# An fnet-plus-gMLP block in split fp32: a new opening for the first three x tiles, three mod rows spread by fp32r products, and the last operands' chain overlapped

## The chip, the cores and the metric

The kernel runs on one core of one Trainium2 chip. The metric is the device time of one execution in microseconds (us), the median of three runs. One further execution is recorded by the hardware profiler; all positions in time below are in us from the start of that execution's span.

## The reference, cut to what matters

```python
mod = (silu(c) @ w_mod).reshape(1, 6, 1, 512)        # w_mod: 512 x 3072
sa, ca, ga, sb, cb, gb = mod rows 0..5
h = layernorm(x) * (1 + ca) + sa                     # x: 2048 x 512
a = h @ dft_hid_re.T;  b = h @ dft_hid_im.T          # 512 x 512 each
x = x + ga * (dft_seq_re @ a - dft_seq_im @ b)       # 2048 x 2048 each
h = layernorm(x) * (1 + cb) + sb
z = gelu(h @ w_in);  z1, z2 = halves of z            # 512 x 1792
g = w_sp @ layernorm(z2) + b_sp[:, None]             # w_sp: 2048 x 2048
out = x + gb * ((z1 * g) @ w_out)                    # w_out: 896 x 512
```

Everything is fp32.

## The kernel before

Each large fp32 product is made of three fp32r products: an operand is split into a high part (`hi`, a copy rounded to fp32r on ScalarE) and a low part (`lo`, the difference, on VectorE), and `matmul3` sums hi x hi, lo x hi and hi x lo in one PSUM bank. Lines L79, L80 and L81 are these three products; each streams 512 columns against a 128 x 128 stationary block.

The large matrices arrive as blocks of 512 x 512 (`stage`, 1 MB, two buffers, loaded by four DMAs of SyncE's queue). A quarter of a block is called a step here, and numbered n. For step n, `prep_hi` makes the transposed tile `t` on VectorE (L142) and `ah` on ScalarE (L165), and `prep_lo` makes `al` on VectorE (L174). `prep(n)` runs three steps ahead with the hi part and two steps ahead with the lo part. There are two `t`, four `ah` and three `al` buffers, so an `al` for step n waits until TensorE has ended step n - 3.

In the first pass (steps 0 to 31) a step is 12 products of 128 x 512: `gp<-ah,hh`, `gp<-al,hh` and `gp<-ah,hl` for each of four banks. `hh` and `hl` are the hi and lo part of one tile of 128 rows of the modulated layernorm, called tile s below (in the profile `x`, `xn`, `hh`, `hl` with its number). Steps 0 to 3 use tiles 0 to 3 with the cosine block, steps 4 to 7 the same tiles with the sine block, steps 8 to 11 and 12 to 15 tiles 4 to 7, and so on: a new group of four tiles is needed from steps 8, 16 and 24 on, one tile a step.

Such a tile goes through `stats_x` (mean and variance on VectorE, L87 and L89; then three small operations on GpSimd, L91, L92 and L99), `norm_x` (ScalarE, L103), `scale_x` (times mod row 1, L255), `shift_x` (plus mod row 0, L258), `hi_h` (ScalarE, L266) and `lo_h` (VectorE, L271). For tiles 4 to 15 the scale and the shift run on GpSimd.

The six mod rows are sums over four chunks of w_mod (`wm`, 128 x 512 each). Rows 1 and 0 are needed first and are summed by fp32 products with `scb` (silu(c) spread over 128 columns, L225). The others are summed on VectorE by `sum_mod`, and `make_mod` (L231) spreads the sum over all partitions by one fp32 product with `ones`; the profile records such a product as two instructions. `keep_mod` (L207) copies the row out of PSUM.

In the last stage the gate `g` (L464) is added and multiplied into `u` (L466, on GpSimd for even f and on VectorE for odd f), split into `uh` and `ul` (L75, L76), and multiplied with `wo` into four banks `op`, for f from 0 to 6: 12 products each.

The order on every engine is the order in which the code issues it (no scheduler moves it). `at(n, f, ...)` queues a call that `run(n)` makes after step n's products were issued. An engine works its instructions off in that order, so one that waits holds up what stands behind it.

Of the kernel before, what the change touches and what calls it, by code (L numbers as in the profile page):

```python
# [19 lines left out]
def fnet_gmlp_kernel(  # L20
# [45 lines left out]
    def bank(k, name):  # L66
        return psum.tile([P, 512], F32, tag=f"bank{k}", bufs=1, name=name)
# [5 lines left out]
    def split(hi, lo, src):  # L73

        nc.scalar.activation(hi, src, AF.Copy)  # L75
        nc.vector.tensor_tensor(lo, src, hi.bitcast(F32), op=ALU.subtract)  # L76
# [30 lines left out]
    def at(n, f, *a):  # L107
        fill.setdefault(n, []).append((f, a))
# [44 lines left out]
    def prep_hi(n):  # L153
        if n >= NE:
            return
        b, k = divmod(n, 4)
        T[n] = blocks.tile([P, Q], F32, tag="t", bufs=2, name=f"t{n}")
        if N3 <= n < N4:

            nc.vector.transpose(T[n].rearrange("p (k a i) -> p a k i", k=4, i=32),  # L160
                                stage[b][:, :, 32 * k:32 * k + 32].rearrange("p (a k) i -> p a k i", k=4))
        else:
            squares(T[n], stage[b], k)
        AH[n] = blocks.tile([P, Q], F32R, tag="ah", bufs=4, name=f"ah{n}")
        nc.scalar.activation(AH[n], T[n], AF.Copy)  # L165
        if k == 3:
            stage.pop(b)
            load(b + 2)

    def prep_lo(n):  # L170
        if n >= NE:
            return
        AL[n] = blocks.tile([P, Q], F32R, tag="al", bufs=3, name=f"al{n}")
        nc.vector.tensor_tensor(AL[n], T.pop(n), AH[n].bitcast(F32), op=ALU.subtract)  # L174
# [17 lines left out]
    sc = cpool.tile([P, ND], F32, name="sc")  # L192
    nc.scalar.activation(sc, ccol, AF.Silu)
    scb = spool.tile([P, ND, P], F32, name="scb")
    for k in range(ND):
        nc.vector.tensor_scalar(scb[:, k, :], ones, sc[:, k:k + 1], None, op0=ALU.mult)
    wm, mods = {}, {}

    def load_mod(j):
        wm[j] = [SP[-1].tile([P, D], F32, tag=f"wm{k}", bufs=2 if len(SP) == 1 else 1, name=f"wm{j}_{k}") for k in range(ND)]  # L200
        for k in range(ND):
            nc.sync.dma_start(wm[j][k], w_mod[k * P:(k + 1) * P, j * D:(j + 1) * D])

    def keep_mod(j, ps, pl, plus_one):
        if j not in mods:
            mods[j] = pl.tile([P, D], F32, name=f"mod{j}")
        nc.scalar.activation(mods[j], ps, AF.Copy, bias=1.0 if plus_one else 0.0)  # L207

    def sum_mod(j, ks=range(4), pl=None):
        w = wm[j]  # L210
        for k in ks:
            if k == 0:
                nc.vector.tensor_scalar(w[0], w[0], sc[:, 0:1], None, op0=ALU.mult)
            else:
                d = w[0]
                if k == 3 and pl:
                    d = mods[j] = pl.tile([P, D], F32, name=f"mod{j}")
                nc.vector.scalar_tensor_tensor(d, w[k], sc[:, k:k + 1], w[0], op0=ALU.mult, op1=ALU.add)

    def sum_mod_first(j, k, pl, plus_one):  # L220

        ps = bank(k, f"modp{j}")
        w = wm.pop(j)
        for m in range(ND):
            nc.tensor.matmul(ps, scb[:, m, :], w[m], start=m == 0, stop=m == ND - 1)  # L225
# [10 lines left out]
    def load_x(g, ks=range(4)):  # L236

        if g not in XG:
            XG[g] = spool.tile([P, 4, D], F32, tag="x", bufs=2, name=f"x{g}")
        k0, k1 = ks[0], ks[-1] + 1  # L240
        v = x.rearrange("(g a k i) d -> g a i k d", g=NQ, a=4, i=32)
        for a in range(4):
            nc.sync.dma_start(XG[g][32 * a:32 * a + 32, k0:k1, :], v[g, a][:, k0:k1, :])
        for k in ks:
            X[4 * g + k] = XG[g][:, k, :]

    def stats_x(s):
        NRM[s] = norm([X[s]], "x")

    def norm_x(s):  # L250
        LN[s] = spool.tile([P, D], F32, tag="xn", bufs=4, name=f"xn{s}")
        apply(LN[s], X.pop(s), NRM.pop(s))

    def scale_x(s, eng=nc.vector):
        eng.tensor_tensor(LN[s], LN[s], mods[1], op=ALU.mult)  # L255

    def shift_x(s, eng):
        eng.tensor_tensor(LN[s], LN[s], mods[0], op=ALU.add)  # L258
# [5 lines left out]
    def hi_h(s):  # L264
        h_hi[s] = hpool.tile([P, ND, P], F32R, name=f"hh{s}")
        nc.scalar.activation(*parts_h(s, h_hi), AF.Copy)  # L266

    def lo_h(s):
        h_lo[s] = hpool.tile([P, ND, P], F32R, name=f"hl{s}")
        lo, h = parts_h(s, h_lo)  # L270
        nc.vector.tensor_tensor(lo, h, parts_h(s, h_hi)[0].bitcast(F32), op=ALU.subtract)  # L271
        LN.pop(s)
# [229 lines left out]
            mm([n])  # L502


    load_x(0, range(2))
    load_mod(1)
    load_mod(0)
    load(0)
    load_x(0, range(2, 4))
    load(1)  # L510
    load_x(1)
    stats_x(0)
    stats_x(1)
    norm_x(0)
    norm_x(1)
# [12 lines left out]
    prep_lo(1)
    lo_h(1)
    stats_x(2)  # L530
    stats_x(3)
    norm_x(2)
    norm_x(3)
    scale_x(2)
    shift_x(2, nc.gpsimd)
# [195 lines left out]
```

## Time and profile before

| | us |
|---|---|
| median of three runs | 1011.55 (1011.09 to 1011.59) |
| the profiled execution, its time | 1010.55 |
| the profiled execution, its span | 1008.8 |
| outside the span | 1.75 |
| first product of step 0 | 18.47 |
| first product of the last stage | 983.99 |
| last product | 1004.42 |

A timeline row gives the start and the duration in us, the engine (PE is TensorE's matmul, PEld its weight load, DVE VectorE, ACT ScalarE, POOL GpSimd, SPq SyncE's DMA queue), the line, the operation, output and inputs, and in brackets how long the engine had been idle and what ended that wait. The durations of neighbouring matmuls overlap, so the pace of TensorE is read from start to start.

### The profile page before, as it was taken

How to read it: one execution, taken by the hardware profiler on the slowest of the kernel's cores; microseconds unless marked ns; L12 is line 12 of the kernel's file. 1: busy time of each engine (PE TensorE's matmuls, PEld its weight loads, DVE VectorE, ACT ScalarE, POOL GpSimd, SP SyncE). 2: the span in 40 equal slices, each digit the busy share in tenths (PEclk: the TensorE clock that was granted, in tenths of full speed). 3: DMA queues.
4: the chain of work that ended last, by engine and by line, in shares of the span. 5: the costliest groups of instructions: out<-in, count | busy, mean ns of one | idle time of the engine just before them, and what ended most of it. 6: DMA issues, size and time to landing. Idle time of an engine off the chain costs nothing.

```text
span 1008.8 us, 11594 instructions
## 1 busy us (share of the span) xinstructions
PE 989.4 (98%) x4344; PEld 817.5 (81%) x4344; DVE 530.6 (53%) x810; ACT 293.0 (29%) x447; POOL 177.3 (18%) x285
## 2 busy tenths in 40 slices
PE   5899999999999999999999999999999999999998
PEld 3678888788888888888888998888888888888886
DVE  4777874666565545647432676565332632263315
ACT  2444441322232313222442675431111111111101
POOL 2677002022310023004321112102000200020001
PEclk9999999999999999999999999999999999999999
DMA  9674962565354353555553232425225222521141
GB/s 241 134 168 106 207 150 70 136 157 146 94 125 97 81 136 105 123 117 156 181 201 142 42 67 60 115 60 150 72 62 157 53 63 66 154 68 48 42 136 42
DMA packets 145961, 114.28 MB, mean 113 GB/s; under 512 B 7024, under 2 KB 125808, under 8 KB 145904
## 3 DMA queue, kind: packets, MB, share of 16 engines
q1 hardware_dynamic: 139296, 93.61, 39.7%
q0 software_dynamic: 6080, 19.93, 5.4%
q8 instruction: 34, 0.56, 0.2%
q14 instruction: 23, 0.19, 0.1%
q10 hardware_dynamic: 528, 0.00, 0.0%
HBM read 93.59 MB, written 19.92 MB: 113 GB/s over the span
## 4 chain that ended last, share of the span: by engine, by line
PE 90%; POOL 4%; DVE 2%; issue 1%; ACT 1%; DMA 0%; SPq 0%; POOLq 0%; DVEq 0%; ACTq 0%
PE gw L79 10%; PE gw L81 10%; PE gw L80 10%; PE gp L81 10%; PE gp L80 10%; PE gp L79 10%; PE yp L81 3%; PE yp L80 3%; PE yp L79 3%; PE z2p L80 3%; PE z2p L79 3%; PE z2p L81 3%; PE z1p L79 3%; PE z1p L81 3%; PE z1p L80 3%; PE op L81 2%
## 5 line engine op out<-in xcount | busy, mean ns | idle before, releaser
L165 ACT ACTIVATE ah<-t 128x512 fp32r<-128x512 f32 x224 | 141.4, 631 | 547.7 <-PE gw L81 212.2
L174 DVE TENSOR_TENSOR al<-t,ah 128x512 fp32r<-128x512 f32 x224 | 156.1, 697 | 271.8 <-PE gw L80 142.3
L79 PE MATMUL gp<-ah,hh 128*128 128x512 f32 x512 | 202.7, 396 | 7.1 <-ACT ah L165 4.1
L80 PE MATMUL gp<-al,hh 128*128 128x512 f32 x512 | 201.3, 393 | 2.2 <-DVE al L174 2.2
L81 PE MATMUL gp<-ah,hl 128*128 128x512 f32 x512 | 200.8, 392 | 0.2 <-DVE hl L271 0.2
L81 PE MATMUL gw<-ah,zl 128*128 128x512 f32 x448 | 174.5, 389 | 0.0
L80 PE MATMUL gw<-al,zh 128*128 128x512 f32 x448 | 174.5, 389 | 0.0
L79 PE MATMUL gw<-ah,zh 128*128 128x512 f32 x448 | 174.5, 389 | 0.0
L142 DVE STREAM_TRANSPOSE t<-stage 128x512 f32<-128x512 f32 x208 | 146.3, 703 | 5.1 <-DMA stage<-in_A_dft_seq_re_dram 1.5
L79 PEld LDWEIGHTS gp<-ah,hh 128*128 128x128 f32 x512 | 96.9, 189 | 29.5 <-ACT ah L165 4.9
L80 PEld LDWEIGHTS gp<-al,hh 128*128 128x128 f32 x512 | 97.0, 189 | 24.6 <-DVE al L174 4.1
L81 PEld LDWEIGHTS gp<-ah,hl 128*128 128x128 f32 x512 | 97.0, 189 | 21.2 <-DVE hl L271 1.3
L81 PEld LDWEIGHTS gw<-ah,zl 128*128 128x128 f32 x448 | 84.1, 188 | 17.6
L80 PEld LDWEIGHTS gw<-al,zh 128*128 128x128 f32 x448 | 84.1, 188 | 17.4
L79 PEld LDWEIGHTS gw<-ah,zh 128*128 128x128 f32 x448 | 84.1, 188 | 17.3
L466 POOL TENSOR_TENSOR u<-u,g 128x512 f32<-128x512 f32 x16 | 20.7, 1291 | 343.4 <-DVE g L464 343.4
L337 POOL DMA_DIRECT2D x_d<-xr x16 | 8.8, 548 | 246.6 <-DVE xr L336 246.6
L81 PE MATMUL yp<-hth,gl 128*128 128x512 f32 x128 | 49.9, 389 | 0.0
L79 PE MATMUL yp<-hth,gh 128*128 128x512 f32 x128 | 49.8, 389 | 0.0
L80 PE MATMUL yp<-htl,gh 128*128 128x512 f32 x128 | 49.8, 389 | 0.0
L80 PE MATMUL z2p<-wil,ah 128*128 128x448 f32 x128 | 46.8, 366 | 0.0
L81 PE MATMUL z2p<-wih,al 128*128 128x448 f32 x128 | 46.8, 366 | 0.0
(94 smaller groups left out, 1158.4 us busy)
## 6 DMA issues: line engine op xcount, KB each, us to landing
stage<-in_A_dft_seq_re_dram SPq DMA_DIRECT2D x64, 256.0 KB, 5.1
stage<-in_A_dft_seq_im_dram SPq DMA_DIRECT2D x64, 256.0 KB, 5.1
stage<-in_B_w_sp_dram SPq DMA_DIRECT2D x64, 256.0 KB, 4.9
stage<-h_d SPq DMA_DIRECT2D x32, 256.0 KB, 4.7
z_d<-z POOLq DMA_DIRECT2D x28, 256.0 KB, 5.8
u<-z_d SPq DMA_DIRECT2D x4, 1792.0 KB, 8.0
wm<-in_w_mod_dram SPq DMA_DIRECT2D x24, 256.0 KB, 4.6
xr<-in_A_x_dram POOLq DMA_DIRECT2D x16, 256.0 KB, 3.3
```

Of the source, the lines that this page charges most:

```text
L79: nc.tensor.matmul(acc, ah, bh, start=first, stop=False)
L80: nc.tensor.matmul(acc, ah, bl, start=False, stop=False)
L81: nc.tensor.matmul(acc, al, bh, start=False, stop=last)
L142: nc.vector.transpose(dst.rearrange("p (b i) -> p b i", i=32), block[:, :, 32 * k:32 * k + 32])
L165: nc.scalar.activation(AH[n], T[n], AF.Copy)
L174: nc.vector.tensor_tensor(AL[n], T.pop(n), AH[n].bitcast(F32), op=ALU.subtract)
L337: nc.gpsimd.dma_start(x2_d[t][i * P:(i + 1) * P, :], x2)
L466: eng.tensor_tensor(U[t][:, f, :], U[t][:, f, :], g, op=ALU.mult)
```

## The change

The diff does five things.

1. The first DMA brings three x tiles instead of two. Tiles 0, 1 and 2 go together through statistics, `norm_x`, scale and shift, all four shifts and scales on VectorE; tile 3 is made by `make_x` out of two fused operations on VectorE (with its own statistics), without ScalarE and GpSimd's wide operations.
2. Mod row 0 is summed in part on VectorE: three of its chunks by `sum_mod`, the fourth by TensorE with `scb`, and the VectorE sum is added by a product with `ones`. Two products of constants stand on TensorE ahead of mod row 1 and three behind mod row 0 (`keep_busy`); nothing reads their output.
3. From tile 4 on the statistics start at the steps of the list `begin`, most of them unchanged, those of tiles 4 to 7 one or two steps later; the scale and shift are issued with `norm_x` instead of a step later, and hi and lo three steps after the statistics.
4. Mod rows 4, 3 and 5 are split into hi and lo (`split_mod`) and spread by two fp32r products (`spread_mod`) instead of one fp32 product. Mod row 2 keeps `make_mod`.
5. In the last stage the gate, the multiplication and `uh` of f + 1 are issued ahead of `ul` and the products of f.

```diff
-    def sum_mod_first(j, k, pl, plus_one):
+    def sum_mod_first(j, k, pl, plus_one, summed=0):
 
         ps = bank(k, f"modp{j}")
         w = wm.pop(j)
-        for m in range(ND):
-            nc.tensor.matmul(ps, scb[:, m, :], w[m], start=m == 0, stop=m == ND - 1)
+        for m in range(summed, ND):
+            nc.tensor.matmul(ps, scb[:, m, :], w[m], start=m == summed, stop=not summed and m == ND - 1)
+        if summed:
+            nc.tensor.matmul(ps, ones, w[0], start=False, stop=True)
+        keep_mod(j, ps, pl, plus_one)
+
+    def keep_busy(n, k):
+
+        ps = bank(k, "busyp")
+        for _ in range(n):
+            nc.tensor.matmul(ps, ones, busy, start=True, stop=True)
+
+    def split_mod(j):
+        w = wm[j][0]
+        wm[j] = [SP[-1].tile([P, D], F32R, tag=f"ws{i}", bufs=1, name=f"ws{j}_{i}") for i in range(2)]
+        split(*wm[j], w)
+
+    def spread_mod(j, k, pl, plus_one):
+
+        ps = bank(k, f"modp{j}")
+        hi, lo = wm.pop(j)
+        nc.tensor.matmul(ps, ones_r[0], hi, start=True, stop=False)
+        nc.tensor.matmul(ps, ones_r[0], lo, start=False, stop=True)
         keep_mod(j, ps, pl, plus_one)
...
+    def make_x(s):
+
+        mean, rstd = stats([X[s]], "x")
+        LN[s] = spool.tile([P, D], F32, tag="xn", bufs=4, name=f"xn{s}")
+        nc.vector.scalar_tensor_tensor(LN[s], X.pop(s), mean, mods[1], op0=ALU.subtract, op1=ALU.mult)
+        nc.vector.scalar_tensor_tensor(LN[s], LN[s], rstd, mods[0], op0=ALU.mult, op1=ALU.add)
...
-    load_x(0, range(2))
+    load_x(0, range(3))
     load_mod(1)
     load_mod(0)
     load(0)
-    load_x(0, range(2, 4))
+    load_x(0, range(3, 4))
     load(1)
     load_x(1)
...
+    keep_busy(2, 5)
...
+    sum_mod(0, range(3))
     sum_mod_first(1, 7, spool, True)
-    sum_mod_first(0, 6, spool, False)
-    scale_x(0)
+    sum_mod_first(0, 6, spool, False, 3)
+    keep_busy(3, 5)
...
-    for s in range(4, NS):
-        at(max(2 * s - 9, 2), stats_x, s)
-        at(max(2 * s - 8, 3), norm_x, s)
-        at(max(2 * s - 7, 3), scale_x, s, nc.gpsimd)
-        at(max(2 * s - 7, 3), shift_x, s, nc.gpsimd)
-        at(max(2 * s - 5, 4), split_h, s)
+    begin = [3, 4, 5, 7, 9, 11, 13, 15, 17, 19, 21, 22]
+    for s, n in zip(range(4, NS), begin):
+        at(n, stats_x, s)
+    for s, n in zip(range(4, NS), begin):
+        at(n + 1, norm_x, s)
+        at(n + 1, scale_x, s, nc.gpsimd)
+        at(n + 1, shift_x, s, nc.gpsimd)
+        at(n + 3, split_h, s)
...
+        at(n + 2, split_mod, j)
-        at(n + 4, make_mod, j, k, cpool if j == 5 else htpool, plus_one)
+        at(n + 4, spread_mod, j, k, cpool if j == 5 else htpool, plus_one)
...
-    for f in range(NF):
+    def first_part(f):
         make_u(t, f)
         uh[f] = blocks.tile([P, Q], F32R, tag="ah", bufs=4, name=f"uh{f}")
+        nc.scalar.activation(uh[f], U[t][:, f, :], AF.Copy)
+
+    first_part(0)
+    for f in range(NF):
+        if f + 1 < NF:
+            first_part(f + 1)
         ul[f] = blocks.tile([P, Q], F32R, tag="al", bufs=3, name=f"ul{f}")
-        split(uh[f], ul[f], U[t][:, f, :])
+        nc.vector.tensor_tensor(ul[f], U[t][:, f, :], uh[f].bitcast(F32), op=ALU.subtract)
```

How the order moves, first on VectorE at the start, from the first scale (before) and from the last two sums of mod row 0 (changed) on. `xn1` is tile 1, `mod1` a mod row, `wm0_0` the running sum of mod row 0, `t0` and `al0` belong to step 0. Before:

```order
L255 TENSOR_TENSOR xn0_171<-xn0_171,mod1_180 128x512
L258 TENSOR_TENSOR xn0_171<-xn0_171,mod0_187 128x512
L255 TENSOR_TENSOR xn1_173<-xn1_173,mod1_180 128x512
L271 TENSOR_TENSOR hl0_195<-xn0_171,hh0_193 128x512
L142 STREAM_TRANSPOSE t0_197<-stage0_134 128x512
L174 TENSOR_TENSOR al0_201<-t0_197,ah0_199 128x512
L142 STREAM_TRANSPOSE t1_203<-stage0_134 128x512
L174 TENSOR_TENSOR al1_209<-t1_203,ah1_205 128x512
L271 TENSOR_TENSOR hl1_211<-xn1_173,hh1_207 128x512
```

The same place with the change:

```order
L220 SCALAR_TENSOR_TENSOR wm0_0_128<-wm0_1_129,sc_106,wm0_0_128 128x512
L220 SCALAR_TENSOR_TENSOR wm0_0_128<-wm0_2_130,sc_106,wm0_0_128 128x512
L278 TENSOR_TENSOR xn0_185<-xn0_185,mod1_199 128x512
L278 TENSOR_TENSOR xn1_187<-xn1_187,mod1_199 128x512
L278 TENSOR_TENSOR xn2_189<-xn2_189,mod1_199 128x512
L281 TENSOR_TENSOR xn0_185<-xn0_185,mod0_204 128x512
L281 TENSOR_TENSOR xn1_187<-xn1_187,mod0_204 128x512
L301 TENSOR_TENSOR hl0_219<-xn0_185,hh0_214 128x512
L281 TENSOR_TENSOR xn2_189<-xn2_189,mod0_204 128x512
L301 TENSOR_TENSOR hl1_222<-xn1_187,hh1_217 128x512
L142 STREAM_TRANSPOSE t0_224<-stage0_136 128x512
L174 TENSOR_TENSOR al0_228<-t0_224,ah0_226 128x512
```

Between the copy of mod row 0 and `t0`, five wide operations stand where three stood; the shifts of tiles 1 and 2 are among them, where before GpSimd made them.

Second, on VectorE around `al8`, the lo operand of step 8. Before:

```order
L271 TENSOR_TENSOR hl4_401<-xn4_355,hh4_399 128x512
L142 STREAM_TRANSPOSE t8_405<-stage2_247 128x512
L174 TENSOR_TENSOR al7_409<-t7_372,ah7_374 128x512
L271 TENSOR_TENSOR hl5_425<-xn5_359,hh5_423 128x512
L87 BN_STATS bstx_429<-x1_148 128x6
L89 BN_AGGR mvx_431<-bstx_429 128x2
L142 STREAM_TRANSPOSE t9_438<-stage2_247 128x512
L174 TENSOR_TENSOR al8_442<-t8_405,ah8_407 128x512
```

With the change:

```order
L142 STREAM_TRANSPOSE t8_393<-stage2_258 128x512
L174 TENSOR_TENSOR al7_397<-t7_353,ah7_355 128x512
L87 BN_STATS bstx_411<-x1_150 128x6
L89 BN_AGGR mvx_413<-bstx_411 128x2
L142 STREAM_TRANSPOSE t9_424<-stage2_258 128x512
L174 TENSOR_TENSOR al8_428<-t8_393,ah8_395 128x512
L301 TENSOR_TENSOR hl4_444<-xn4_389,hh4_442 128x512
L142 STREAM_TRANSPOSE t10_450<-stage2_258 128x512
L174 TENSOR_TENSOR al9_454<-t9_424,ah9_426 128x512
L87 BN_STATS bstx_468<-x1_150 128x6
L89 BN_AGGR mvx_470<-bstx_468 128x2
L301 TENSOR_TENSOR hl5_479<-xn5_420,hh5_477 128x512
```

`al8` stood behind `hl5`, and now stands ahead of `hl4`.

Third, on VectorE in the last stage (`g3_1` is the gate of f = 1, `ul0` the lo part of f = 0). Before:

```order
L464 TENSOR_TENSOR g3_0_7696<-gw3_0_7148,bs3_7576 128x512
L76 TENSOR_TENSOR ul0_7700<-u3_7574,uh0_7699 128x512
L464 TENSOR_TENSOR g3_1_7715<-gw3_1_7149,bs3_7576 128x512
L466 TENSOR_TENSOR u3_7574<-u3_7574,g3_1_7715 128x512
L76 TENSOR_TENSOR ul1_7719<-u3_7574,uh1_7718 128x512
L464 TENSOR_TENSOR g3_2_7738<-gw3_2_7150,bs3_7576 128x512
```

With the change:

```order
L494 TENSOR_TENSOR g3_0_7720<-gw3_0_7172,bs3_7600 128x512
L494 TENSOR_TENSOR g3_1_7725<-gw3_1_7173,bs3_7600 128x512
L496 TENSOR_TENSOR u3_7598<-u3_7598,g3_1_7725 128x512
L731 TENSOR_TENSOR ul0_7730<-u3_7598,uh0_7723 128x512
L494 TENSOR_TENSOR g3_2_7744<-gw3_2_7174,bs3_7600 128x512
L731 TENSOR_TENSOR ul1_7749<-u3_7598,uh1_7728 128x512
```

The gate of f + 1 moves ahead of the lo part of f, throughout the stage.

More of the change, by code (lines that the diff above doesn't have):

```diff
@@ L194, in fnet_gmlp_kernel @@
     scb = spool.tile([P, ND, P], F32, name="scb")
+    busy = spool.tile([P, D], F32, name="busy")
+    nc.vector.memset(busy, 1.0)
     for k in range(ND):
@@ L508, in fnet_gmlp_kernel @@
     load(0)
-    load_x(0, range(2, 4))
+    load_x(0, range(3, 4))
     load(1)
     load_x(1)
[L512 to L515, printed above, removed]
+    keep_busy(2, 5)
+    for s in range(3):
+        stats_x(s)
+    for s in range(3):
+        norm_x(s)
+    sum_mod(0, range(3))
     sum_mod_first(1, 7, spool, True)
-    sum_mod_first(0, 6, spool, False)
-    scale_x(0)
+    sum_mod_first(0, 6, spool, False, 3)
+    keep_busy(3, 5)
+    for s in range(3):
+        scale_x(s)
     shift_x(0, nc.vector)
-    scale_x(1)
-    shift_x(1, nc.gpsimd)
     hi_h(0)
+    shift_x(1, nc.vector)
+    hi_h(1)
     lo_h(0)
+    shift_x(2, nc.vector)
+    lo_h(1)
     prep_hi(0)
     prep_lo(0)
+    hi_h(2)
     prep_hi(1)
-    hi_h(1)
     prep_lo(1)
[L529 to L535, printed above, removed]
+    lo_h(2)
+    make_x(3)
     prep_hi(2)
-    scale_x(3)
-    shift_x(3, nc.gpsimd)
-    at(0, split_h, 2)
     at(0, hi_h, 3)
@@ L556, in change_pools @@
         load_ht(1)
+    ones_r = []
     def change_spool():
@@ L561, in change_spool @@
         load_mod(4)
+        ones_r.append(SP[-1].tile([P, P], F32R, name="ones_r"))
+        nc.scalar.activation(ones_r[0], ones, AF.Copy)
     at(14, load_mod, 2)
```

## The prediction

> **What bounds the kernel.** I read the page, then the waits, then the timeline of TensorE alone.
>
> ```profile
> PE 989.4 (98%) x4344; PEld 817.5 (81%) x4344; DVE 530.6 (53%) x810; ACT 293.0 (29%) x447; POOL 177.3 (18%) x285
> ```
>
> TensorE is busy for 98% of the span, so only three things can save time: a wait of TensorE, a stretch at its lower clock, or a product that costs less. Its waits (engine and line, what it waited for: total us, times, longest):
>
> ```profile
> PE modp L225 <- DMA wm<-in_w_mod_dram: 5.8, 1, 5.8
> PE gp L79 <- ACT ah L165: 4.1, 1, 4.1
> PE gp L79 <- ACT hh L266: 3.0, 1, 3.0
> PE gp L80 <- DVE al L174: 2.2, 3, 1.3
> ```
>
> All of them are in the opening. The next rows are TensorE's there: the mod sums, the first product of steps 0, 2, 3 and 8, the second of step 8, the first and third of step 11, and the first of steps 12, 19 and 28.
>
> ```profile
> 5.82 8.56 PE L225 MATMUL modp<-wm,scb 128*128 128x512 f32 x16 [5.82 <-DMA wm<-in_w_mod_dram]
> 18.47 0.49 PE L79 MATMUL gp<-ah,hh 128*128 128x512 f32 x1 [4.08 <-ACT ah L165]
> 29.21 0.79 PE L79 MATMUL gp<-ah,hh 128*128 128x512 f32 x1 [2.99 <-ACT hh L266]
> 33.67 0.39 PE L79 MATMUL gp<-ah,hh 128*128 128x512 f32 x1
> 47.29 0.39 PE L79 MATMUL gp<-ah,hh 128*128 128x512 f32 x1
> 49.03 0.50 PE L80 MATMUL gp<-al,hh 128*128 128x512 f32 x1 [1.34 <-DVE al L174]
> 57.23 0.50 PE L79 MATMUL gp<-ah,hh 128*128 128x512 f32 x1
> 58.12 0.50 PE L81 MATMUL gp<-ah,hl 128*128 128x512 f32 x1 [0.15 <-DVE hl L271]
> 60.52 0.39 PE L79 MATMUL gp<-ah,hh 128*128 128x512 f32 x1
> 79.56 0.39 PE L79 MATMUL gp<-ah,hh 128*128 128x512 f32 x1
> 104.44 0.39 PE L79 MATMUL gp<-ah,hh 128*128 128x512 f32 x1
> ```
>
> Undisturbed, a step takes (79.56 - 60.52) / 7 = 2.72 us, or 0.2267 a product. Step 2 lasts 4.46 instead, step 8 loses 1.5, step 11 takes 3.29 (0.57 lost), and steps 19 to 27 lose 104.44 - 79.56 - 9 x 2.72 = 0.40. The clock explains step 2 (columns: window, length, busy us of PE, PEld, DVE, ACT, POOL; granted clock, DMA share, GB/s):
>
> ```profile
> 20.00:22.00 2.00, 2.00 (x6) 1.52 (x6) 1.54 (x3) 0.95 (x2) 0.00 (x0) 0.50 1.21 228
> 26.00:29.00 3.00, 0.22 (x1) 0.00 (x0) 2.61 (x4) 1.92 (x4) 2.07 (x2) 1.00 0.10 25
> 31.00:33.00 2.00, 2.00 (x7) 1.54 (x6) 2.00 (x5) 0.83 (x2) 0.00 (x0) 0.58 1.15 220
> ```
>
> After each long idle time the clock is about half for some 3 to 4 us.
>
> **Part 1, the opening.** The goal is the moment when step 3 can start, 33.67 before. I follow the new chain.
>
> *Mod row 0.* Its last chunk decides. Below are the last two `wm` DMAs (starts of the issue, then time to landing), and DVE's rows at the start.
>
> ```profile
> L202 SPq DMA_DIRECT2D wm<-in_w_mod_dram x2: 430/430/430, 5.4 to 5.9; - x2
> DMA to landing us min/median/max: 5.6/6.0/6.4
> 14.42 0.60 ACT L207 ACTIVATE mod<-modp 128x512 f32<-128x512 f32 x1 [2.84 <-PE modp L225]
> 15.05 0.69 DVE L258 TENSOR_TENSOR xn<-xn,mod 128x512 f32<-128x512 f32 x1 [2.74 <-ACT mod L207]
> 15.66 0.68 DVE L255 TENSOR_TENSOR xn<-xn,mod 128x512 f32<-128x512 f32 x1
> 18.45 0.69 DVE L174 TENSOR_TENSOR al<-t,ah 128x512 fp32r<-128x512 f32 x1 [0.70 <-ACT ah L165]
> 223.52 0.75 DVE L218 SCALAR_TENSOR_TENSOR wm<-wm,sc,wm 128x512 f32<-128x512 f32 x1
> ```
>
> The chunks landed at 11.0 and 12.3. A third x tile stands ahead of them on SP's queue: 262 KB more. At the 228 GB/s of the window from 20 to 22 that is 1.15 us. The two last chunks are 0.26 MB each and landed 1.3 apart, but the six before them came faster: issued 0.43 apart, they landed by 11.0, 1.8 MB and 0.5 MB of x in the 9 us from 2 on, 260 GB/s or 1.0 us; some of that time is latency. I take 0.75, between none and 1.15: the last chunk lands at 13.05. VectorE's sum is ready at 11.75 + 0.75 = 12.5, in time. Two fp32 products follow on TensorE, 0.87 each at full clock (part 2): 1.7, and 0.15 to the last product's end, on which the copy waits. It starts at 14.9 and ends at 15.55, against 15.0 before. So mod row 0 comes 0.5 later, not sooner. Mod row 1, the idle products (covered by the 5.8 us wait for the first chunk, and by the 4 us before step 0) and the three scales all end before that.
>
> *VectorE from 15.55 on.* A wide operation follows the last after 0.61 (15.05 to 15.66); `al0` and `al1` each wait 0.70 for ScalarE. To `t0`: five operations ahead and itself, 6 x 0.61 plus 0.3 for `hh0`, to 19.55. It starts at 18.85, 1.8 later than before (18.45 less 0.70 and its own 0.70), so block 0, which the extra tile delays by at most 1.15 on SP's queue, is covered; the blocks and tiles behind it on that queue keep their sum of bytes. `al0` ends 1.4 later, `t1` and `al1` another 2.0: 22.95. Then `hl2`, the statistics of tile 3 (0.61 + 0.69 + 0.18), two fused operations (1.5), `t2`, `t3` and `al2` (1.95): 27.95. TensorE starts step 0 at 20.3 instead of 18.47. Steps 0 and 1 took 7.6 us from there to the end in the trace, at half clock, so they end at 27.9, and at full clock at about 25.9. In both cases `al2` lets step 2 go on at 28.0, now without the 3 us idle time ahead. Step 3 starts at 28.0 + 11 x 0.2267 = 30.5: **3.2 sooner.**
>
> *Step 8.* `al8` waited behind `hl5`, which waited for tile 5 from GpSimd. It now stands ahead of `hl4`; the 1.5 us go. Step 11 would start at 30.5 + 8 x 2.72 = 52.25.
>
> *Step 11 and after.* Tile 7's lo part is next to be late, through GpSimd.
>
> ```profile
> 35.80 0.55 POOL L92 TENSOR_TENSOR rsx<-mvx,mhalf 128x1 f32<-128x1 f32 x1
> 67.30 1.30 POOL L255 TENSOR_TENSOR xn<-xn,mod 128x512 f32<-128x512 f32 x1 [0.93 <-ACT xn L103]
> 68.67 1.62 POOL L258 TENSOR_TENSOR xn<-xn,mod 128x512 f32<-128x512 f32 x1
> 70.66 0.89 POOL L92 TENSOR_TENSOR rsx<-mvx,mhalf 128x1 f32<-128x1 f32 x1
> 72.83 1.29 POOL L255 TENSOR_TENSOR xn<-xn,mod 128x512 f32<-128x512 f32 x1 [0.93 <-ACT xn L103]
> ```
>
> One tile takes GpSimd 5.53 (67.30 to 72.83): 3.0 for scale and shift, 1.1 to 1.5 for the small operations, 0.9 waiting for ScalarE. Tile 5's statistics stand behind `al6`, which waits for the end of step 3 (33.2): GpSimd has them at 34.9 and, as its order puts both small chains ahead of tile 4's scale, is through with tile 4 at 39.0, with tiles 5 and 6 at 46.1 (one small chain, two wide pairs), with tile 7 at 51.2; up to 52.2 if every L92 takes 0.89. `hh7` and `hl7` add 1.4: 52.6 to 53.6, against 52.7 when step 11's third product is due. The loss is 0 to 0.95; I take 0.5, near the 0.57 of before. Step 12 then starts at 52.25 + 2.72 + 0.5 = 55.5, which is 5.0 sooner. From there four tiles cost GpSimd 22.1 and TensorE 21.8, so at steps 19 and 27 up to 0.36 is lost each, 0.7 against 0.40 before. **The opening gives 4.7.** Ends: 3.5 (the 1.2 us load, and 0.95 at step 11) and 5.7 (no later load, no loss at step 11).
>
> **Part 2, three mod rows.** The product before, the mod product, and the second product after it; then `al` of step 51.
>
> ```profile
> 190.40 0.39 PE L81 MATMUL gp<-ah,hl 128*128 128x512 f32 x1
> 190.63 1.02 PE L231 MATMUL modp<-wm,ones 128*128 128x512 f32 x2
> 191.72 0.39 PE L80 MATMUL gp<-al,hh 128*128 128x512 f32 x1
> 188.58 0.65 DVE L174 TENSOR_TENSOR al<-t,ah 128x512 fp32r<-128x512 f32 x1
> ```
>
> The row costs 1.32 - 2 x 0.2267 = 0.87. Two fp32r products of the usual shape cost 0.45, so 0.41 is saved, three times: **1.2** (none, if a split came late). Each split adds 0.6 to ScalarE and 0.7 to VectorE. The tightest is the first: `al` of step 51 ended at 189.2 and is used at 191.72, 2.5 us of cover against 0.7 plus as much waiting for ScalarE.
>
> **Part 3, the last stage.** Its first product, two places where TensorE waited, and its last; VectorE's lo part at the first of these places.
>
> ```profile
> 983.99 0.39 PE L79 MATMUL op<-woh,uh 128*128 128x512 f32 x1
> 995.34 0.69 DVE L76 TENSOR_TENSOR ul<-u,uh 128x512 fp32r<-128x512 f32 x1 [2.07 <-ACT uh L75]
> 995.36 0.50 PE L79 MATMUL op<-woh,uh 128*128 128x512 f32 x1
> 1001.51 0.50 PE L79 MATMUL op<-woh,uh 128*128 128x512 f32 x1
> 1004.42 0.39 PE L81 MATMUL op<-woh,ul 128*128 128x512 f32 x1
> ```
>
> 84 products need 83 x 0.2267 = 18.8 from first to last; they took 20.4. VectorE has five operations for two f (3.4 us) while TensorE has 24 products (5.4), so issued one f ahead the chain gate, GpSimd, `uh`, `ul` keeps up; what remains is TensorE. I take **1.4** of the 1.6; ends 0.8 (half) and 1.6. The additions and stores behind the last product stay as they are.
>
> **Sum.** 4.7 + 1.2 + 1.4 = 7.3. The profiled execution goes from 1010.55 to 1003.25. The median of the runs shown lies 1.0 above it, so I predict 1004.3.
>
> [...] The clock decides the two fp32 products of mod row 0: at half clock they take 3.4 instead of 1.7. TensorE is idle ahead of them from the end of mod row 1 (four products of 0.87 from 5.82 + 0.75 on, at full clock to 10.05; a chunk may hold up the last one a little) to 13.05, at most 3.0 us. The trace: 2.99 us of idle time were enough for the half clock from 29.21 on. [...]
>
> **Rivals.** *Half clock at mod row 0.* For it speaks the 2.99 us that were enough at 29.21; against it, that the window from 26 to 29 still shows a clock of 1.00, so the drop came only at the very end of that idle time. Everything up to step 28 comes 1.7 later: 1006.0.
>
> *The opening is no sooner.* The change delays step 0, and if `al2` came at 31.1 instead of 27.95 step 3 would start at 33.67 again. That needs 3.2 us more on VectorE, more than any row shows; the reordering at step 8 would still pay. Without the 3.2: 1007.5; without both, 1009.
>
> *Slower: GpSimd becomes the bound.* Before, it was through with tile 11 at 75.8 (72.83 + 3.0), 2.8 ahead of the third product of step 19 less 1.4 for `hh` and `hl`; now it has nothing to spare from tile 7 on. Each 0.1 us on its 5.53 costs 0.8 over the eight tiles from 8 to 15. From 6.45 us a tile on the whole gain is gone; at 6.9 the kernel takes 1015.3. Against it: L92 moved by only 0.34 when other engines were active, and no row of GpSimd's wide operations moved by more.
>
> *Better:* the third tile costs the mod loads nothing and tile 7 is in time: 1003.3 or less.
>
> **Chances.** The forecast (1003.3 to 1005.4) 0.55; half clock 0.23; better 0.12; no sooner 0.07; GpSimd-bound 0.03. The range that leaves out no more than 2 in 10 runs from 1002.4 to 1007.0. A change of 0.2% (2.0 us) is about what a measurement of this kernel can tell from none: faster than that 0.94, same 0.03, slower 0.03.
>
> **What would show it.** Step 0 at about 20.3, step 3 at about 30.5 without a bracketed wait of 3 us ahead of step 2; no wait at step 8; the third product of step 11 behind `hl` L301; two L247/L248 products at 0.23 each; 18.8 to 19.0 from first to last product of the last stage. Wrong would be above all a mod row 0 copied later than 16, an `al2` later than 29, or GpSimd's tiles more than 5.6 apart.

## The result, and the profile after

The changed kernel takes 1003.13 us (median; 1002.91 to 1003.54) against 1011.37 us (1011.09 to 1011.59) for the kernel before on the same chip: ratio 0.9919, 95% interval [0.9902, 0.9936]. The two profiled executions took 1003.15 and 1010.55 us, 7.4 us apart.

The page's first row, and the rows of TensorE's own waits (engine and line, what it waited for: total us, times, longest):

```profile
PE 988.9 (99%) x4350; PEld 818.5 (82%) x4350; DVE 543.1 (54%) x820; ACT 295.9 (30%) x450; POOL 172.9 (17%) x281
PE modp L227 <- DMA wm<-in_w_mod_dram: 3.2, 2, 1.7
PE gp L79 <- ACT ah L165: 2.7, 1, 2.7
```

The wait for `hh` (3.0) ahead of step 2 is gone, and so is the 1.34 us wait for `al` at step 8. Now the timeline of TensorE: the start of mod row 0's two products, the idle products, the first products of steps 0, 2, 3, 9, 10, 11, 12 and 28, the two products of one spread mod row, and the first and last product of the last stage.

```profile
12.21 1.12 PE L227 MATMUL modp<-wm,scb 128*128 128x512 f32 x2 [1.66 <-DMA wm<-in_w_mod_dram]
14.03 2.74 PE L236 MATMUL busyp<-busy,ones 128*128 128x512 f32 x6
19.48 0.80 PE L79 MATMUL gp<-ah,hh 128*128 128x512 f32 x1 [2.72 <-ACT ah L165]
28.27 0.39 PE L79 MATMUL gp<-ah,hh 128*128 128x512 f32 x1
30.99 0.39 PE L79 MATMUL gp<-ah,hh 128*128 128x512 f32 x1
47.31 0.39 PE L79 MATMUL gp<-ah,hh 128*128 128x512 f32 x1
50.03 0.39 PE L79 MATMUL gp<-ah,hh 128*128 128x512 f32 x1
53.26 0.50 PE L79 MATMUL gp<-ah,hh 128*128 128x512 f32 x1 [0.35 <-ACT hh L296]
56.41 0.39 PE L79 MATMUL gp<-ah,hh 128*128 128x512 f32 x1
99.98 0.39 PE L79 MATMUL gp<-ah,hh 128*128 128x512 f32 x1
186.13 0.39 PE L247 MATMUL modp<-ws,ones_r 128*128 128x512 f32 x1
186.36 0.39 PE L248 MATMUL modp<-ws,ones_r 128*128 128x512 f32 x1
978.19 0.39 PE L79 MATMUL op<-woh,uh 128*128 128x512 f32 x1
997.00 0.39 PE L81 MATMUL op<-woh,ul 128*128 128x512 f32 x1
```

Read against the rows of before: step 3 starts 2.68 us sooner (33.67 to 30.99), step 9 4.34 sooner (51.65 to 47.31: step 8's stall is gone), step 12 4.11 sooner (60.52 to 56.41), step 28 4.46 sooner. A spread row is two products of 0.227 us, 0.455 in all, against 0.87. The last stage takes 18.81 from first to last product instead of 20.43. That is nearly the whole difference of 7.4 us: 4.46 + 3 x 0.415 + 1.62 = 7.3.

The row that matters most is the one at 28.27. It has no bracket: TensorE came to step 2 busy. The third `al` had ended at 27.60, 0.67 earlier (first row), and the clock tells why TensorE was late (columns as in the windows of before; the clock is the third number from the end):

```profile
26.91 0.69 DVE L174 TENSOR_TENSOR al<-t,ah 128x512 fp32r<-128x512 f32 x1
19.00:19.50 0.50, 0.02 (x1) 0.02 (x1) 0.04 (x1) 0.50 (x2) 0.00 (x0) 0.64 1.27 227
20.00:25.00 5.00, 5.00 (x12) 3.84 (x12) 3.79 (x8) 0.63 (x1) 1.05 (x2) 0.50 1.07 224
25.50:26.00 0.50, 0.50 (x3) 0.41 (x2) 0.50 (x2) 0.00 (x0) 0.00 (x0) 0.53 0.09 25
```

Half clock lasted from 19.14 to 25.97 (0.64 is the mean of the window from 19.00 to 19.50, so its first 0.14 us were at full clock; the end in the same way), and steps 0 and 1 took 8.79 us (19.48 to 28.27). In that stretch products follow each other 0.43 us apart (21.23, 21.65, 22.08), behind it 0.227. The prediction had reckoned with 7.6 at the most, and with `al2` as the bound.

### The profile page after: what moved, and what is told of

Its sections match the earlier page's. It is cut to its first block, busy times and chain, and to the rows that moved or that the text cites. A ratio compares the mean times of both kernels' runs of the same rounds, so it can differ in the third digit from the quotient of the medians.

```text
span 1001.4 us, 11608 instructions
## 1 busy us (share of the span) xinstructions
PE 988.9 (99%) x4350; PEld 818.5 (82%) x4350; DVE 543.1 (54%) x820; ACT 295.9 (30%) x450; POOL 172.9 (17%) x281
## 4 chain that ended last, share of the span: by engine, by line
PE 94%; POOL 2%; issue 1%; DVE 1%; DMA 1%; ACT 0%; SPq 0%; DVEq 0%; POOLq 0%
PE gp L81 11%; PE gp L80 11%; PE gp L79 10%; PE gw L79 10%; PE gw L81 10%; PE gw L80 10%; PE yp L81 3%; PE yp L80 3%; PE yp L79 3%; PE z2p L80 3%; PE z2p L79 3%; PE z2p L81 3%; PE z1p L79 3%; PE z1p L80 3%; PE z1p L81 3%; PE op L81 2%
## 5 line engine op out<-in xcount | busy, mean ns | idle before, releaser
L174 DVE TENSOR_TENSOR al<-t,ah 128x512 fp32r<-128x512 f32 x224 | 161.6, 721 | 271.6 <-PE gw L80 142.6
L79 PE MATMUL z2p<-wih,ah 128*128 128x448 f32 x128 | 46.7, 365 | 0.0
```

The costliest lines, as they stand in the source:

```text
L79: nc.tensor.matmul(acc, ah, bh, start=first, stop=False)
```

## Experiments

First theory, the prediction's: VectorE's chain from mod row 0 to `al2` lets step 2 go on, whatever the clock is; beside it, the order at step 8 and GpSimd at step 11. Second theory, from the trace after: TensorE at half clock bounds steps 0 to 2, with `al2` right behind it. Each kernel was timed beside the kernel before, whose median moved between 1011.37 and 1012.11; each ratio's interval is about 0.0015 (1.5 us) to either side, so that for differences of 1 or 2 us between two changed kernels the traces decide and the times only agree or not.

### The three parts by themselves

`open_only` is the change without the spread rows and without the new last stage; `mod_only` and `tail_only` are the kernel before with one of these.

> Only the opening of the change (three x tiles first, mod row 0 partly summed on VectorE, idle products, the new order up to step 19); mod rows 3 to 5 and the last stage as before. By the prediction's terms, as the changed kernel's trace corrects them: the opening gives 4.5 of 7.4 us, so 1.2 + 1.6 = 2.8 above the changed kernel: 1005.9. If the parts hide each other (what comes sooner at step 28 waits again later): less far above it, 1004 to 1005.

> Only the three mod rows of the change (split into two fp32r tiles and spread by two products); the opening and the last stage as before. By the rows of the two traces a spread row costs TensorE 0.455 instead of 0.87 us: 3 x 0.41 = 1.2 less than the kernel before, 1010.2, and the two rows of each pair stand 0.23 apart without a wait. If the splits hold up the operands' chain on VectorE once the opening's 4.5 us have not moved the work there: a wait ahead of the pairs and less than 1.2.

> Only the last stage of the change (the chain of the next f issued one f ahead); the opening and the mod rows as before. By the rows of the two traces 1.6 us: 1011.4 - 1.6 = 1009.8. If the last stage's gain needs the work that the other parts moved: no change, 1011.4.

Measured: `open_only` 1005.80 us (ratio 0.9940 [0.9927, 0.9952]), `mod_only` 1010.33 (0.9988 [0.9979, 0.9998]), `tail_only` 1009.80 (0.9982 [0.9973, 0.9990]). The savings 6.0, 1.2 and 1.8 thousandths add up to 9.0, against 8.1 for the whole, within the intervals: as far as these times can tell, the parts neither need nor hide each other. The rows give the small ones more exactly. The first product of a spread row of `mod_only` and the product behind the row, 0.46 later without a wait; then the ends of the last stage of `tail_only`, 18.82 apart:

```profile
191.09 0.39 PE L237 MATMUL modp<-ws,ones_r 128*128 128x512 f32 x1
191.55 0.39 PE L79 MATMUL gp<-ah,hh 128*128 128x512 f32 x1
984.84 0.39 PE L79 MATMUL op<-woh,uh 128*128 128x512 f32 x1
1003.66 0.39 PE L81 MATMUL op<-woh,ul 128*128 128x512 f32 x1
```

### The clock or `al2`: two edits, alone and together

`long_busy`:

```diff
     sum_mod_first(0, 6, spool, False, 3)
-    keep_busy(3, 5)
+    keep_busy(6, 5)
```

`early_al2`:

```diff
     prep_hi(0)
+    prep_hi(1)
     prep_lo(0)
     hi_h(2)
-    prep_hi(1)
     prep_lo(1)
     lo_h(2)
-    make_x(3)
     prep_hi(2)
+    at(0, make_x, 3)
     at(0, hi_h, 3)
```

`early_long` is both.

> The changed kernel with six idle products instead of three behind mod row 0 (twelve halves of 0.43 us instead of six, about 14.0 to 19.2 us). First theory, the prediction's: the third al (al2, ended at 27.60) lets step 2 go on, whatever the clock is; then this kernel takes the time of the changed kernel, 1003.1, give or take 0.3. Second theory, from the changed kernel's trace: TensorE's half clock from 19.5 to 25.9 us made steps 0 and 1 take 8.79 us and bounds step 2 itself; with the clock up step 2 waits only for ah2 and al2 (26.9 and 27.6), step 3 starts at about 30.1 instead of 30.99, 0.9 sooner: 1002.3. Third: the steps at full clock end at 25.0, TensorE then idles for 2.4 us before step 2 and loses the clock there, where 2.72 us of idle time were enough for it before step 0; step 2 at half clock takes 5.4 us, step 3 starts at 32.8 or later, 1.8 later: 1004.9.

> The changed kernel with VectorE's opening in another order: t0 and t1 ahead of al0 and al1 (which takes away its two waits of 0.70 us for ScalarE), and t2, t3 and al2 ahead of the statistics and the two fused operations of tile 3. By the durations of the changed kernel's rows al2 then ends at about 24.8 us instead of 27.60, and the hi and lo parts of tile 3 at about 28.2 and 29.5. Idle products as in the changed kernel. First theory (al2 bounds step 2, the clock does not): step 2 goes on 2 us or more sooner; step 3 then waits for tile 3 and starts at 28.6 to 29.2 instead of 30.99: about 1001. Second theory (TensorE at half clock bounds steps 0 and 1): step 2 still starts at about 28.2 and, at a full clock from 25.9 on, step 3 at 30.9: 1003.1, or up to 0.8 less where step 1 no longer waits for al1.

> Both edits together: six idle products instead of three behind mod row 0, and VectorE's opening reordered so that al2 ends at about 24.8 us. Second theory (both the half clock and, right behind it, al2 bound the opening): neither edit alone brings more than 0.9, both together bring more than the sum: step 0 at 19.5, steps 0 and 1 at full clock to 25.0, step 2 to 27.7, step 3 from 28.3 with its third product behind the lo part of tile 3 at 29.5: step 4 at about 31.6 instead of 33.7, 2.1 sooner, so 1001.0 (1001.9 if tile 7 on GpSimd then loses another 0.9 at step 11). First theory (the clock does not matter): the same as with the reordering alone, about 1001.

Measured: `long_busy` 1002.81 (0.9912), `early_al2` 1003.12 (0.9909), `early_long` 1001.43 (0.9897 [0.9883, 0.9912]). By the medians neither edit alone moves the time by more than 0.3 us from the changed kernel's 1003.13, both together by 1.7; by the ratios (0.9919 for the changed kernel) it is 0.7 and 1.0 us alone and 2.2 together, which the intervals do not separate. The traces do: against the changed kernel step 3 starts 0.34 us sooner in `long_busy`, 0.20 later in `early_al2` and 1.44 sooner in `early_long`. In `early_al2` the third `al` ends at 23.6, four us sooner, and step 3 starts no sooner, since steps 0 and 1 ran at half clock again (0.50 in the windows from 19.5 to 25; first fence: that `al`, the first products of steps 0 and 3). In `long_busy` they run at full clock (1.00 in every window from 11 to 33), and then TensorE waits for `ah`, and behind it `al`, of step 2 (second fence: steps 0, 2 and 3).

```profile
22.93 0.69 DVE L174 TENSOR_TENSOR al<-t,ah 128x512 fp32r<-128x512 f32 x1
19.74 0.80 PE L79 MATMUL gp<-ah,hh 128*128 128x512 f32 x1 [3.04 <-ACT ah L165]
31.19 0.39 PE L79 MATMUL gp<-ah,hh 128*128 128x512 f32 x1
```

```profile
19.59 0.50 PE L79 MATMUL gp<-ah,hh 128*128 128x512 f32 x1
27.29 0.49 PE L79 MATMUL gp<-ah,hh 128*128 128x512 f32 x1 [1.48 <-ACT ah L165]
30.65 0.39 PE L79 MATMUL gp<-ah,hh 128*128 128x512 f32 x1
```

In `early_long` steps 0 to 2 take 8.81 us instead of 11.51 (first products of steps 0 and 3):

```profile
20.74 0.50 PE L79 MATMUL gp<-ah,hh 128*128 128x512 f32 x1 [0.23 <-ACT ah L165]
29.55 0.39 PE L79 MATMUL gp<-ah,hh 128*128 128x512 f32 x1
```

So the second theory holds: two limits end within 0.7 us of each other at step 2, and removing either one uncovers the other. The prediction's number for step 2 (28.0) came out, its "in both cases" did not. Which limit shows is a matter of the run: in the profile of `open_only`, whose opening is that of the changed kernel, the clock stayed up (1.00 in every window from 17 to 28; step 1 at 22.84, step 2 waiting for `ah` at 26.89, step 3 at 30.28). One of the four times of `early_al2`, 1001.53, lies with those of `early_long`. It has no profile, but its mean granted clock is on record as 0.998, against 0.997 for the other three: the profiled executions of `t4_only` and `best2`, with one stretch of 3.4 us at half clock, have 0.998, those of the changed kernel and of `no_busy`, with 6.8 us, 0.997, so that a shorter stretch is likely. The profiled execution of `early_long` (1001.86) gained 1.3 us, less than the 2.1 expected, because mod row 1 ran at the pace of half clock there nearly to its end: its first seven instructions last some 0.85 us from start to start instead of 0.43, and it takes 6.65 us (6.99 to 13.64) instead of 3.67. Mod row 0 is then copied at 15.40 instead of 14.22, and step 0 starts at 20.74 instead of 19.48. (The expectation of `best2` below has 5.46 us and four instructions for this; 5.46 is the time of the first six alone.) The clock column doesn't show it: in this trace it reads 1.00 from 11 to 13 too, where the products still keep that pace.

### The idle products, and the sum of mod row 0

`no_busy` takes both `keep_busy` calls and their tile out. `row0_te` sums mod row 0 on TensorE alone:

```diff
-    sum_mod(0, range(3))
     sum_mod_first(1, 7, spool, True)
-    sum_mod_first(0, 6, spool, False, 3)
+    sum_mod_first(0, 6, spool, False)
```

> The changed kernel without its two stretches of idle products and the tile that they read; nothing that the output needs is left out. If the idle products bring a good part of the gain: mod row 1 is at half clock for its first four instructions (1.7 us later at its end, in front of nothing, since mod row 0's last chunk lands at 12.1), and the products of mod row 0, at half clock too, come 1.7 us later, and all up to step 28 with them: 1004.8. If they bring nothing: mod row 0 runs at full clock because mod row 1, now longer, ends closer to it, as before the change; step 0 starts at half clock as it does with them: 1003.1, give or take 0.3.

> The changed kernel with mod row 0 summed wholly on TensorE, as before the change, instead of three of its four chunks on VectorE. By the changed kernel's rows the last chunk lands at about 12.1 us; TensorE then has one product of 0.87 left instead of two, so mod row 0 is copied about 0.9 sooner, at 13.3 instead of 14.22. First theory (VectorE's chain and TensorE's half clock bound the opening, and VectorE has the three scales to do until 14.5 in any case): VectorE waited 0.36 for the copy, so at most 0.4 less: 1002.7 to 1003.2. Second theory (the sum on VectorE is what lets step 0 start in time): TensorE reaches the last product late, step 0 starts 1 to 2 us later: 1004 to 1005.

Measured: `no_busy` 1003.21 (0.9914): as they stand, the idle products bring nothing that the times show; in the changed kernel three of them end 2.72 us ahead of step 0, and half clock still follows, from 19.14. `row0_te` 1004.19 (1002.86 to 1005.77; 0.9929): 1.1 us slower in the median and more scattered. In its profiled execution, the longest of the five (1005.77), mod row 0 is copied at 17.21 instead of 14.22 (of the eleven instructions in the first row, three belong to mod row 1):

```profile
11.53 5.65 PE L227 MATMUL modp<-wm,scb 128*128 128x512 f32 x11
17.21 0.60 ACT L209 ACTIVATE mod<-modp 128x512 f32<-128x512 f32 x1 [2.84 <-PE modp L227]
```

Mod row 1 came late on TensorE there (its first seven instructions last some 0.85 us from start to start instead of 0.43), and four products of mod row 0 instead of two stood behind it. My first expectation, that the last chunk's landing decides and TensorE would have one product left, missed this. In `early_long` mod row 1 was as late (its last instruction starts at 13.05, here at 13.15), but with the sum on VectorE mod row 0 was copied at 15.40, 1.81 us sooner. So the part of the sum on VectorE makes the opening less dependent on TensorE's clock. The 1.1 us between the medians are within the intervals of the two ratios.

### Step 8: the order of tiles 4 to 15

`old_begin` puts the old places back. They differ for every tile: in the list `begin` the statistics of all tiles from 4 to 15, not only of 4 to 7, start one or two steps later than before. (`...` stands for lines left out.)

```diff
-    begin = [3, 4, 5, 7, 9, 11, 13, 15, 17, 19, 21, 22]
-    ...
+    for s in range(4, NS):
+        at(max(2 * s - 9, 2), stats_x, s)
+        at(max(2 * s - 8, 3), norm_x, s)
+        at(max(2 * s - 7, 3), scale_x, s, nc.gpsimd)
+        at(max(2 * s - 7, 3), shift_x, s, nc.gpsimd)
+        at(max(2 * s - 5, 4), split_h, s)
```

> The changed kernel with the old places in the order for tiles 4 to 15 (statistics at step 2s - 9 and so on), so hl4 and hl5 stand ahead of al8 again, and GpSimd gets the tiles one to two steps sooner. First theory, the prediction's: the order at step 8 is what removed its stall of 1.5 us; the stall comes back, step 11 then loses less than its 0.94, about 0.6 us more in all: 1003.7. Second theory: the stall went because GpSimd no longer has tiles 1 to 3, so tiles 4 and 5 come some 3 us sooner whatever the order; nothing is lost at step 8, and tile 7 comes in time for step 11: 0.9 less, 1002.2.

Measured: 1006.73 (0.9947), 3.6 us slower than the changed kernel by the medians and 2.8 by the ratios, more than either theory had. Rows of VectorE and TensorE: the lo part of tile 5, the `al` behind it, and step 8's first two products.

```profile
45.47 0.78 DVE L301 TENSOR_TENSOR hl<-xn,hh 128x512 fp32r<-128x512 f32 x1 [3.05 <-ACT hh L296]
47.58 0.65 DVE L174 TENSOR_TENSOR al<-t,ah 128x512 fp32r<-128x512 f32 x1
45.30 0.39 PE L79 MATMUL gp<-ah,hh 128*128 128x512 f32 x1
48.29 0.50 PE L80 MATMUL gp<-al,hh 128*128 128x512 f32 x1 [2.60 <-DVE al L174]
```

The stall is back, and larger than the 1.34 of before, since TensorE now reaches step 8 2 us sooner. The profiled execution (1007.37) has two losses more. After the stall of 2.60 us the clock was at half from 49.37 to 52.78, which costs 1.7 us by my estimate, half of that time:

```profile
49.00:49.50 0.50, 0.50 (x4) 0.41 (x3) 0.50 (x1) 0.45 (x1) 0.02 (x1) 0.87 0.00 0
52.50:53.00 0.50, 0.50 (x3) 0.36 (x3) 0.50 (x2) 0.00 (x0) 0.42 (x1) 0.72 0.00 0
```

And the fourth chunk of mod row 0 came 1.1 us later than in the changed kernel (its product starts at 13.35 instead of 12.21), which left step 3 0.71 later. Two other executions, of 1006.71 and 1006.73, have a mean granted clock of 1.000, so by that figure the median stands without such a stretch; how its 3.6 us divide isn't shown. GpSimd was through with tile 5 at 41.9 in this run, so having fewer tiles ahead of it does not save step 8: ScalarE's norm of tile 6 stands ahead of `hh5` and holds it to 44.75. The new order is what the opening's gain needs to get past step 8.

### Step 11: GpSimd

`t4_only` finishes tile 4 with VectorE's two fused operations (statistics in step 3, `make_x`'s last two lines in step 4) instead of ScalarE's norm and GpSimd's scale and shift.

> The changed kernel with one edit: tile 4 is finished by VectorE's two fused operations (1.5 us) instead of ScalarE's norm and GpSimd's scale and shift (3.0 us). If GpSimd is what makes step 11 lose 0.94 us in the changed kernel (tile 7's shift ends at 52.54, hh7 and hl7 follow): tile 7 comes up to 3 us sooner, the loss goes, 1002.2. If the loss has another cause, or VectorE becomes late in its turn: 1003.1 or more.

In the changed kernel, tile 7's scale and shift on GpSimd and its hi part on ScalarE (the lo part follows on VectorE at 53.24), then the next tile's L92 and scale:

```profile
49.87 1.30 POOL L278 TENSOR_TENSOR xn<-xn,mod 128x512 f32<-128x512 f32 x1 [0.94 <-ACT xn L103]
51.24 1.30 POOL L281 TENSOR_TENSOR xn<-xn,mod 128x512 f32<-128x512 f32 x1
52.58 0.63 ACT L296 ACTIVATE hh<-xn 128x512 fp32r<-128x512 f32 x1 [0.43 <-POOL xn L281]
53.23 0.55 POOL L92 TENSOR_TENSOR rsx<-mvx,mhalf 128x1 f32<-128x1 f32 x1
55.08 1.30 POOL L278 TENSOR_TENSOR xn<-xn,mod 128x512 f32<-128x512 f32 x1 [0.94 <-ACT xn L103]
```

Measured for `t4_only`: 1002.03 (0.9906), 1.1 less than the changed kernel. Its tile 7 ends on GpSimd at 51.48 (50.19 + 1.29) instead of 52.54, 1.06 us sooner and not the 3 us allowed for, and steps 10 and 11 lose 0.31 instead of 0.94 (first products of steps 10, 11 and 12):

```profile
49.58 0.39 PE L79 MATMUL gp<-ah,hh 128*128 128x512 f32 x1
52.30 0.40 PE L79 MATMUL gp<-ah,hh 128*128 128x512 f32 x1
55.33 0.39 PE L79 MATMUL gp<-ah,hh 128*128 128x512 f32 x1
```

GpSimd is the cause, as the prediction said: ScalarE's `hh` of tile 7 waited for it (0.43 us in the changed kernel's row), and TensorE for that `hh`. It accounts for 0.63 of the 1.1; the other 0.45 stood ahead already at step 3 (30.54), where this run's clock came back sooner (half clock from 20.43 to 23.85).

### Towards a faster version

`best2` joins `early_long` and `t4_only`, with three idle products instead of two at the start. `best3` adds idle products that read the finished tile 2 and `t0`, so that they reach up to step 0, and starts tile 5 one step earlier on GpSimd.

> The reordering and the longer second stretch of idle products together, as in the run before (which lost 1.2 us to a mod row 1 at half clock in its first four instructions, 5.46 us against 3.67), with two more edits: three idle products instead of two ahead of mod row 1, and tile 4 finished by VectorE's two fused operations (1.5 us) in place of ScalarE's and GpSimd's (3.0 us there), so that GpSimd is through with tile 7 sooner. If both reasons hold: mod row 1 at full clock, t0 back at about 18.1 us and step 3 at 28.3 instead of 30.99; nothing lost at step 11 instead of 0.94: 1003.1 - 2.7 - 0.9 = 999.5. If VectorE then becomes late at steps 4 to 8, where its extra 1.5 us stand ahead of al7: about 1000.5 to 1001. If the loss at step 11 has another cause than GpSimd: 1000.4.

> The kernel of the run with tile 4 on VectorE (1001.0), in whose trace TensorE idled for 1.45 us ahead of step 0 and fell to half clock at 21.2 us, so that step 0 took 4.94 us instead of 2.72 and step 3 started at 30.53. Edits: five idle products instead of six, then one that reads the finished tile 2 (ready at about 18.1) and half a one that reads t0 (ready at about 19.4), so that the idle time ahead of step 0 is under 1 us in pieces; and the norm, scale and shift of tile 5 stand one step earlier. If the half clock is what holds steps 0 to 2 there: steps 0 and 1 take 5.4 us, step 3 starts at about 28.4 behind the parts of tile 3, 2.1 sooner; of that GpSimd gives back about 0.6 to 1.4 at step 11: 999.5 to 1000.3. If idle pieces of under 1 us are enough to lose the clock, or the idle products come late and push step 0: 1001 or more.

Measured: `best2` 1001.01 (0.9893 [0.9879, 0.9906]), `best3` 1001.05 (0.9896 [0.9881, 0.9912]): both faster than the changed kernel by 2.1 us. The 0.4 to `early_long` are within the intervals, and both fall short of what was expected, `best2` by 1.5 us and `best3` by 0.8 to 1.5. In the profiled execution of `best2`, its longest (1001.77), the loss at step 11 is gone (it takes 2.80 us, to 55.09), but the idle products ended 1.45 us ahead of step 0 and half clock came after all, from 21.63 to 25.04 (step 0, step 1, and the windows in which the clock fell and rose):

```profile
20.11 0.49 PE L79 MATMUL gp<-ah,hh 128*128 128x512 f32 x1 [1.45 <-ACT ah L165]
25.05 0.41 PE L79 MATMUL gp<-ah,hh 128*128 128x512 f32 x1
21.50:22.00 0.50, 0.50 (x3) 0.43 (x2) 0.50 (x2) 0.00 (x0) 0.00 (x0) 0.63 1.12 238
25.00:25.50 0.50, 0.50 (x3) 0.39 (x2) 0.50 (x1) 0.00 (x0) 0.42 (x2) 0.96 1.03 193
```

That explains only this execution: the other three (1000.27 to 1001.02) have a mean granted clock of 1.000, against 0.998 here, so by that figure they had no such stretch, and missed 999.5 all the same.

The profiled execution of `best3` is its longest, 1003.07; the other three took 1000.89 to 1001.10. It shows the rival "half clock at mod row 0" in part: 2.50 us of idle time ahead of that row's first product, then 1.80 instead of 1.02 for its second one, and the copy at 16.21 instead of 14.22.

```profile
13.41 1.12 PE L227 MATMUL modp<-wm,scb 128*128 128x512 f32 x2 [2.50 <-DMA wm<-in_w_mod_dram]
14.38 1.80 PE L229 MATMUL modp<-wm,ones 128*128 128x512 f32 x2
16.21 0.60 ACT L209 ACTIVATE mod<-modp 128x512 f32<-128x512 f32 x1 [3.44 <-PE modp L229]
```

That execution is 2.1 us slower than the other three, but half clock (0.50 in the window from 15 to 17) is the smaller part of it: of the 1.99 us at the copy, 1.20 come from the chunk, whose product starts at 13.41 instead of 12.21, and 0.78 from the second product. The rival had been priced at 1.7, for both products. What the other runs of `best2` and `best3` wait for isn't shown, as none of them has a profile; the mean granted clock of those of `best3`, 0.999 to 1.000, leaves no room for a recorded stretch of 3.4 us at half clock, with which `best2` and `t4_only` have 0.998.

## Why the prediction came out

The sum against the profiled execution was 7.3, and 7.4 was measured; the 1.2 us between 1004.3 and 1003.13 are nearly all the last step, where I put the median 1.0 above the profiled execution because it lay so before. After, the profiled execution (1003.15) lies at the median. That puts 1003.13 just under the forecast's own band (1003.3 to 1005.4), at the time of the rival "better", of whose two conditions one held (the chunk was not delayed) and the other did not (tile 7 was late). By terms:

- *Mod row 0.* The third x tile was to delay the last chunk by 0.75 us; it arrived at about 12.1, as before (12.3). The copy started at 14.22 instead of 14.9, step 0 at 19.48 instead of 20.3. The lower end (no delay) was the right one in this execution. It is not a constant: with the same first DMAs the fourth chunk's product starts at 11.54 in `best2` and at 13.35 and 13.41 in `old_begin` and `best3`. That the clock would be up for the row's two products was my estimate: no run shows up to which idle time it holds. Measured, they took 2.01 us up to the copy after 1.66 us of idle time in the changed kernel, and 2.80 after 2.50 in `best3`.
- *Step 3: 3.2 predicted, 2.68 measured.* The step that failed is "Steps 0 and 1 ... end at 27.9 at half clock ... in both cases `al2` lets step 2 go on": it took 7.6 us over from a trace in which half clock ended after 3.4 us, where here it lasted 6.8. `al2` ended at 27.60 (27.95 predicted), so that part of the chain was right; in `long_busy`, where the clock stayed up, TensorE waited for it at step 2, 0.23 us behind the 1.48 for `ah`.
- *Step 8: 1.5 predicted, 1.66 measured*, by the cause that was given: `old_begin` brings the stall back.
- *Step 11: 0.5 predicted, 0.94 measured*, the upper end; GpSimd was through with tile 7 at 52.54, where the prediction had 51.2 to 52.2; TensorE waited at the first product of the step, for `hh`, before the third was due. `t4_only` shows the cause.
- *Steps 19 and 27: 0.7 predicted, 0.05 measured.* From step 12 to step 28 TensorE takes 43.57 us, 16 x 2.72 = 43.52. The wrong term is L92 at 0.89: it takes 0.55 from tile 7 on. The scales of tiles 7 to 11 start at 49.87, 55.08, 60.76, 65.96 and 71.64, so GpSimd's cycle is 5.2 and 5.7 by turns, 5.44 in the mean instead of 5.53, and no longer than two steps.
- *Mod rows: 1.2 predicted, 3 x 0.415 measured. Last stage: 1.4 predicted, 1.62 measured*; nothing but TensorE was left there.

The misses of -0.5, +0.15, -0.45, +0.65 and +0.2 cancel; that the total is better than its terms is luck. Of the rivals, half clock at mod row 0 did not happen in the profiled execution, and `best3` shows that it can; GpSimd as the bound was real at step 11 only.

## What to carry to other kernels

Where two chains meet at one product, undo each alone and both together before naming the bound: here each edit alone moved step 3 by at most 0.3 us and the pair moved it by 1.4. Idle products that ended well ahead of the real work did not settle the clock here: with 2.72 us between, the changed kernel lost it, and with 2.81 `open_only`, with the same opening, kept it. Those of `early_long` end 0.23 us ahead, and there it stayed up. When a stall is removed early, follow the gain through every later hand-over (here the order on VectorE and ScalarE at step 8, GpSimd at step 11): without the new order 3.6 us of the median were given back.

## What was unexpected in the hardware

From windows of 0.5 us with a mixed clock, the edges of a stretch of half clock can be worked out. Eight of them: before, 19.01 to 22.42 and 29.25 to 32.66; changed kernel, 19.14 to 25.97; `no_busy`, 18.07 to 24.90; `best2`, 21.63 to 25.04; `t4_only`, 20.43 to 23.85; `old_begin`, 22.06 to 25.47 and 49.37 to 52.78. Six last 3.41 or 3.42 us, the ones of the changed kernel and of `no_busy` 6.83. In these two TensorE was still idle at the start (for 0.34 us in the changed kernel, to 19.48, and 1.82 in `no_busy`, to 19.89); in the others it was at work throughout, but for 0.19 us in the first of before.

How long TensorE had been idle does not tell here whether the clock falls. It fell after 1.45 us in `best2`, 2.60 at the stall of `old_begin`, 2.72 in the changed kernel, 2.99 and 4.08 before, and 5.38 in `no_busy`; it stayed at 1.00 after 1.48 us in `long_busy` and after 2.81 in `open_only`. The nearest pair is `open_only` and `t4_only`, whose openings are the same up to step 0 and whose idle times ahead of it differ by 0.01 us (step 0's first product, then a window behind it; first `open_only`, then `t4_only`):

```profile
19.44 0.50 PE L79 MATMUL gp<-ah,hh 128*128 128x512 f32 x1 [2.81 <-ACT ah L165]
20.00:22.00 2.00, 1.83 (x8) 1.51 (x9) 1.30 (x3) 0.63 (x1) 0.00 (x0) 1.00 1.16 229
19.46 0.50 PE L79 MATMUL gp<-ah,hh 128*128 128x512 f32 x1 [2.80 <-ACT ah L165]
21.00:23.00 2.00, 2.00 (x6) 1.59 (x5) 1.55 (x3) 0.42 (x1) 0.00 (x0) 0.50 1.15 225
```

What decides between them is not shown: no run moved the place of an idle time and kept its length.
